# Sparse attention with a gated feed-forward layer on one core: a third unit with seven products, in-place turns, exponentials over two banks, and a newly drawn order

## The chip, the core and the metric

The kernel runs on one core of a Trainium2 chip. The core has five engines with a queue of instructions each: TensorE (PE in the profile) multiplies matrices into PSUM; VectorE (DVE), ScalarE (ACT) and GpSimd (POOL) work on SBUF, the first two on PSUM as well; SyncE (SP) issues transfers. PSUM has eight banks of 512 f32 numbers in each of 128 partitions. An engine takes its instructions strictly in the order of the program and waits on semaphores for the others.

The metric is the time of one execution on the device in microseconds (us). The kernel before was run three times: 274.62, 275.38 and 276.82 us, median 275.38.

## What is computed

Four sequences of 768 rows, eight heads of 64. Queries see chunks of 32 keys. For each query a bound is worked out for every chunk up to its own, from the minimum and the maximum of the chunk's keys; the six chunks with the largest bounds are kept, and a causal softmax over their keys weights the values. The result, as 3072 rows of 512, goes through a gated layer with 1536 hidden columns.

```python
ub = np.sum(np.maximum(q[..., None, :] * k_min, q[..., None, :] * k_max), axis=-1)
top_chunks = np.argsort(np.where(causal, ub, -1e9), axis=-1)[..., -6:]
scores = np.where(selected & (pos[:, None] >= pos[None, :]), scale * q @ k.T, -1e9)
x = softmax(scores) @ v                      # then heads side by side: 3072 x 512
out = (1 / (1 + np.exp(-(x @ w_gate))) * (x @ w_val)) @ w_out
```

## The kernel before

**Units.** The 3072 rows are taken as eight units u0 to u7 of 384 rows, three blocks of 128 each. u1 is blocks 1 to 3 of the first sequence, u2 its blocks 4 and 5 with the first block of the last sequence, u3 blocks 1 to 3 of the second sequence, and so on; u0 collects the first blocks of the others. A unit goes through these steps, whose names stand in the program's list and in this text:

- Keys and queries, loaded as f32. For u1 and u2 they are turned on TensorE (kn, kT, kt, qn, qT, qf). For sequences 1 to 3 they arrive through four transfers (k00_2 or q10_2: tensor, half, half, sequence), already cut into 32 x 32 squares, so that VectorE only has to transpose each square. For the keys (keys_blocks, L839) and each of four pairs of heads: kx0 and kx1 take minimum and maximum of the squares of the raw keys and transpose at once (L684), k16 casts the raw keys to f16 (POOL, L459), kt transposes the cast (L850), and hk0 and hk1 copy the halves to hk, where the scores read them. For the queries (turn_queries, L858) qf0 and qf1 transpose to a tensor of their own (L866); qm takes the positive part, hq0 and hq1 copy to hq (queries_blocks, L870).
- The choice of chunks (choose, L887): ub is the bounds on TensorE into two banks (even and odd heads), and then, for either bank by itself, ubn (transpose), ubm (bar what is not there), mx0/mx1 (eight largest), ap (compare with the sixth), apt (transpose) on VectorE, and hqm copies that add the mask to the query side, so that the score of a dropped chunk comes out very negative.
- Attention (attend, L944): for each of eight heads two to four banks of scores sc, one exponential exp for each bank (ScalarE, L971), the causal cut cm on the diagonal squares (POOL, L977), the values pv on TensorE, then rz (reciprocal) and x (normalise, L1014) on VectorE. x is turned to xT: for u1 and u2 on TensorE with a copy (xps, xT), for u3 to u7 by a transposing transfer.
- The gated layer (ffn, L1234). Hidden columns are taken as three groups of 512. For u0, u1 and u2 each of the twelve column blocks of gate (g) and of value (v) is four products with 384 moving columns (L1247); tanh on ScalarE and hg on VectorE finish the gate. For u3 to u7 (the table SEVEN, L1141) a group is done as a 2 x 2 block product with seven products in place of eight (by7, L1187): products p1 to p7 of four matmuls with 192 columns each (L1199), into two banks, one called lead and one side. e7 copies p7's bank to SBUF, sd copies lead to side, c21 and c22 (L1214) add sums onto the banks, and each quarter goes to tanh or hg. The seven products need sums of weights, ss0 to ss3 for each group (L1170; ss2 overwrites one quarter of the weights, so every plain product with them must have been done), and differences of the unit's input, tt0 to tt3 (L1183).
- The output product: o0, o1, o2 with 512 columns (L1321) for u0 to u3, seven products of two units' blocks (pair, L1063) for u4 to u7, with sums sw of the hidden columns and tw of the output weights (weight_sums, L1042).

**Order.** Nothing is scheduled at run time. The program holds three lists: ORDER (L96) names every step with its engine and is emitted in that sequence, SLOTS (L267) gives each buffer a place in one SBUF tensor called arena, or a PSUM bank, and TIES (L345) makes single steps of POOL wait for the end of a step of VectorE. The list before has 2097 steps, 731 of them on TensorE, 508 on VectorE, 450 on ScalarE, 281 on POOL and 127 on SyncE, and 203 ties. The steps fl are fillers on TensorE in the first microseconds, whose results nobody reads.

Of the kernel before, what the change touches and what calls it, by code (L numbers as in the profile page):

```python
# [14 lines left out]
NEG = -60000.0  # L15
UNITS = 234
# [123 lines left out]
tanh_u1_6=A cm_u2_2=G v_u1_2=P hg_u1_9=V k11_2=S kcr_1=G osb_u0_2=A exp_u2_2_1=A sc_u2_1_2=P exp_u2_0_2=A exp_u2_3_1=A sc_u2_7_1=P  # L140
qf0_u3_1=V k10_2=S sc_u2_6_2=P pv_u2_4=P hq0_u3_0=G exp_u2_6_2=A hg_u1_7=V qf0_u3_2=V pv_u2_5=P v_u1_10=P v_u1_8=P exp_u2_7_1=A qf0_u3_3=V
qm_u3_0=A cm_u2_6=G exp_u2_1_2=A hg_u1_3=V v_u1_6=P hq1_u3_0=G hg_u1_2=V v_u1_11=P hg_u1_6=V hq1_u3_2=G hg_u1_11=V qm_u3_2=A ub_u3=P
hg_u1_8=V k01_2=S xpsf_3_0=P hq0_u3_2=G hk0_1_3=A ss3_g0=G o0_u1_1=P pv_u2_0=P ubn1_u3=V hk1_1_3=A ubn0_u3=V ubm1_u3=V xpsf_3_1=P
xTf_3_1=A kt_1_1=V mx1_u3=V hk1_1_2=A pv_u2_3=P hk0_1_1=A pv_u2_6=P xTf_3_0=A q00_2=S hg_u1_10=V qf0_u4_0=V pv_u2_2=P o1_u1_1=P v16_1_1=G
pv_u2_1=P pv_u2_7=P hk1_1_1=G ap1_u3=V rz_u2_2=V rz_u2_3=V apt1_u3=V rz_u2_0=V hk0_1_0=G x_u2_3=V rz_u2_1=V ubm0_u3=V o2_u1_1=P o0_u1_0=P
x_u2_2=V hk0_1_2=A o1_u1_0=P x_u2_0=V hqm1_u3_2=A q11_2=S osb_u1_1=A xps_u2_3=P sc_u3_7_1=P xT_u2_3=A exp_u3_7_1=A sc_u3_7_2=P mx0_u3=V
qf0_u4_2=V x_u2_1=V hqm1_u3_0=G sc_u3_4_0=P ap0_u3=V exp_u3_4_0=A v16_1_2=G kx1_2_1=V k16_2_3=G xps_u2_2=P apt0_u3=V xT_u2_2=A kx1_2_2=V
sc_u3_5_0=P exp_u3_7_2=A k16_2_0=G hqm0_u3_2=G q01_2=S o0_u1_2=P sc_u3_6_2=P sc_u3_4_2=P exp_u3_4_2=A sc_u3_6_1=P qf0_u4_1=V qf0_u4_3=V
exp_u3_5_0=A o1_u1_2=P k16_2_2=G exp_u3_6_2=A kx0_2_0=V hqm0_u3_0=G sc_u3_5_2=P kt_2_0=V exp_u3_5_2=A exp_u3_6_1=A xps_u2_1=P q10_2=S
sc_u3_6_0=P cm_u3_5=G sc_u3_4_1=P kt_2_3=V exp_u3_6_0=A cm_u3_6=G sc_u3_7_0=P xps_u2_0=P out_u0_1=S o2_u1_0=P xT_u2_1=A kx0_2_2=V  # L150
o2_u1_2=P kx1_2_3=V v_1_3=S xT_u2_0=A g_u2_2=P sc_u3_1_2=P v_1_4=S exp_u3_4_1=A sc_u3_0_1=P g_u2_11=P exp_u3_7_0=A cm_u3_4=G v_1_0=S
cm_u3_7=G sc_u3_5_1=P osb_u1_2=A exp_u3_1_2=A osb_u1_0=A kx0_2_3=V sc_u3_1_0=P k16_2_1=G hk0_2_3=G tanh_u2_11=A v_u2_0=P v_2_1=S
exp_u3_1_0=A cm_u3_1=G exp_u3_0_1=A exp_u3_5_1=A sc_u3_3_1=P qf1_u4_3=V sc_u3_1_1=P exp_u3_1_1=A exp_u3_3_1=A tanh_u2_2=A g_u2_8=P
hk1_2_0=G out_u1_0=S g_u2_10=P qf1_u4_2=V out_u1_1=S kx1_2_0=V qf1_u4_0=V k01_3=S k11_3=S sc_u3_0_2=P v_u2_10=P qf1_u4_1=V sc_u3_3_2=P
g_u2_9=P tanh_u2_10=A hq1_u4_2=G hg_u2_10=V kx0_2_1=V hq0_u4_2=G exp_u3_0_2=A tanh_u2_8=A g_u2_4=P sc_u3_2_1=P v_u2_8=P qf0_u5_1=V
qm_u4_2=A v16_1_3=G v_u2_9=P sc_u3_3_0=P exp_u3_3_2=A hq1_u4_0=G hg_u2_8=V kcr_2=G tanh_u2_9=A out_u0_2=S hg_u2_9=V sc_u3_0_0=P g_u2_0=P
exp_u3_2_1=A qm_u4_0=A g_u2_5=P v16_1_4=G exp_u3_0_0=A qf0_u5_2=V v16_1_0=G ub_u4=P cm_u3_0=G g_u2_3=P exp_u3_3_0=A hk1_2_3=G qf0_u5_3=V
pv_u3_6=P qf0_u5_0=V tanh_u2_0=A k10_3=S tanh_u2_4=A kt_2_1=V sc_u3_2_0=P v16_2_1=G qm_u5_0=A v_u2_11=P ubn0_u4=V tanh_u2_5=A qm_u5_2=A
ubn1_u4=V exp_u3_2_0=A hq1_u5_0=A hk0_2_1=G g_u2_7=P tanh_u2_3=A ubm0_u4=V out_u1_2=S pv_u3_0=P sc_u3_2_2=P exp_u3_2_2=A hg_u2_0=V
mx0_u4=V kt_2_2=V hq1_u5_2=A pv_u3_4=P pv_u3_1=P ap0_u4=V ubm1_u4=V tanh_u2_7=A hg_u2_11=V pv_u3_7=P apt0_u4=V g_u2_1=P v_1_5=S hq0_u4_0=G  # L160
hk1_2_1=G pv_u3_5=P g_u2_6=P tanh_u2_1=A mx1_u4=V k00_3=S hqm0_u4_2=A rz_u3_3=V v_u2_7=P cm_u3_3=G ub_u5=P hg_u2_7=V ap1_u4=V hk0_2_0=G
hk0_2_2=G tanh_u2_6=A x_u3_3=V sc_u4_2_0=P ubn1_u5=V sc_u4_2_2=P apt1_u4=V hqm0_u4_0=A v_u2_4=P v_u2_5=P rz_u3_2=V exp_u4_2_2=A
sc_u4_2_1=P rz_u3_0=V exp_u4_2_0=A sc_u4_1_1=P exp_u4_2_1=A hk1_2_2=G cm_u3_2=G v_u2_1=P hqm1_u4_2=G v_2_0=S ubn0_u5=V hqm1_u4_0=G
sc_u4_3_2=P sc_u4_6_2=P exp_u4_1_1=A x_u3_0=V hg_u2_1=V q10_3=S v_u2_3=P exp_u4_3_2=A cm_u4_2=G sc_u4_5_3=P sc_u4_7_1=P x_u3_2=V
sc_u4_0_0=P pv_u3_3=P exp_u4_6_2=A hg_u2_4=V hg_u2_3=V exp_u4_7_1=A exp_u4_0_0=A sc_u4_6_0=P exp_u4_5_3=A pv_u3_2=P sc_u4_3_1=P v_u2_2=P
sc_u4_3_0=P hg_u2_5=V sc_u4_0_2=P v_u2_6=P exp_u4_3_1=A exp_u4_6_0=A hq0_u5_2=G mx1_u5=V sc_u4_3_3=P sc_u4_4_1=P exp_u4_0_2=A sc_u4_0_1=P
exp_u4_3_3=A hg_u2_2=V sc_u4_5_0=P xT_u3_0=S exp_u4_3_0=A exp_u4_0_1=A sc_u4_4_3=P hg_u2_6=V rz_u3_1=V o0_u2_2=P sc_u4_1_2=P exp_u4_5_0=A
exp_u4_4_1=A sc_u4_5_1=P exp_u4_5_1=A o1_u2_2=P mx0_u5=V ss0_g1=V sc_u4_2_3=P exp_u4_1_2=A sc_u4_4_0=P ss2_g0=G x_u3_1=V ap0_u5=V
xT_u3_1=S sc_u4_1_3=P exp_u4_4_3=A v16_1_5=G sc_u4_1_0=P o0_u2_1=P k16_3_1=A exp_u4_1_3=A kx0_3_2=V sc_u4_7_2=P ss0_g2=V exp_u4_2_3=A
sc_u4_7_3=P k16_3_2=G o1_u2_1=P exp_u4_7_2=A kx1_3_1=V exp_u4_1_0=A xT_u3_3=S ap1_u5=V apt0_u5=V xT_u3_2=S o0_u2_0=P sc_u4_7_0=P ss1_g2=V  # L170
# [230 lines left out]
def kernel(  # L401
# [1065 lines left out]
```

## Time and profile before

| | |
|---|---|
| median of three runs | 275.38 us |
| profiled execution | 274.87 us |
| its span, first to last instruction | 273.0 us |
| busy: PE, DVE, ACT, POOL | 263.1, 227.3, 208.6, 187.3 us |
| idle time of PE | 9.9 us |
| matmuls | 3094 |

The span is what the profile divides into shares; the 1.9 us around it are in the time and not in the profile. In rows of groups the columns are line, engine, operation, output and inputs, shapes and count, then busy time in us, mean ns of one, and the idle time before with what ended it. A matmul's own duration contains the way through the array, so the pace of a stream is read from rows of the chain, where a row gives start, length and the number of products in it.

### The profile page before, as it was taken

How to read it: one execution, taken by the hardware profiler on the slowest of the kernel's cores; microseconds unless marked ns; L12 is line 12 of the kernel's file. 1: busy time of each engine (PE TensorE's matmuls, PEld its weight loads, DVE VectorE, ACT ScalarE, POOL GpSimd, SP SyncE). 2: the span in 40 equal slices, each digit the busy share in tenths (PEclk: the TensorE clock that was granted, in tenths of full speed). 3: DMA queues.
4: the chain of work that ended last, by engine and by line, in shares of the span. 5: the costliest groups of instructions: out<-in, count | busy, mean ns of one | idle time of the engine just before them, and what ended most of it. 6: DMA issues, size and time to landing. Idle time of an engine off the chain costs nothing.

```text
span 273.0 us, 8339 instructions
## 1 busy us (share of the span) xinstructions
PE 263.1 (96%) x3094; PEld 207.8 (76%) x3094; DVE 227.3 (83%) x654; ACT 208.6 (76%) x451; POOL 187.3 (69%) x287
## 2 busy tenths in 40 slices
PE   6979999999999999999999999999999999999994
PEld 4655658657666667675889878899988999999984
DVE  4789846788989989889989999889898879678861
ACT  6378878669886899899889999989998763665322
POOL 5796744658996799697499974887773556584440
PEclk9979999999999999999999999999999999999999
DMA  6999999999999999912783715130200020022035
GB/s 155 240 292 200 204 214 214 214 184 177 170 204 165 202 257 218 180 33 53 166 133 86 195 31 130 42 95 4 46 14 2 17 46 1 2 78 79 2 119 228
DMA packets 131576, 34.74 MB, mean 127 GB/s; under 512 B 119760, under 2 KB 128464, under 8 KB 131536
## 3 DMA queue, kind: packets, MB, share of 16 engines
q1 hardware_dynamic: 126768, 29.50, 50.8%
q0 software_dynamic: 4768, 4.72, 10.2%
q8 instruction: 24, 0.39, 0.6%
q14 instruction: 16, 0.13, 0.1%
HBM read 30.67 MB, written 6.29 MB: 135 GB/s over the span
## 4 chain that ended last, share of the span: by engine, by line
PE 85%; DVE 4%; DMA 4%; ACT 2%; issue 1%; POOL 1%; SPq 1%; DVEq 0%; ACTq 0%
PE sc_u L960 11%; PE g_u L1247 9%; PE o_u L1321 9%; PE v_u L1247 8%; PE pl_v_u L1199 7%; PE pv_u L993 6%; PE pl_g_u L1199 6%; PE pl_u L1092 6%; PE ps_v_u L1199 5%; PE ps_g_u L1199 4%; PE ps_u L1092 4%; PE ube_u L899 3%; DMA arena<-arena 3%; ACT arena L971 1%; DMA arena<-in_k_dram 1%
## 5 line engine op out<-in xcount | busy, mean ns | idle before, releaser
L971 ACT ACTIVATE arena<-sc_u 128x512 f16<-128x512 f32 (+3 forms) x184 | 90.4, 552 | 7.7 <-PE sc_u L960 6.3
L1082 POOL TENSOR_TENSOR arena<-arena 128x256 f16<-128x256 f16 x44 | 29.1, 682 | 23.6 <-DVE arena L1082 9.7
L977 POOL TENSOR_SCALAR_AFFINE_SELECT arena<-arena 128x384 f16<-128x384 f16 (+1 forms) x56 | 28.2, 515 | 18.5 <-DVE arena L1170 4.4
L1321 PE MATMUL o_u<-wo,arena 128*128 128x512 f16 x144 | 35.3, 379 | 0.0
L1199 PEld LDWEIGHTS <-arena 128*128 128x128 f16 x360 | 30.1, 98 | 1.9
L960 PE MATMUL sc_u<-hqe,hke 128*128 128x128 f16 (+2 forms) x220 | 28.9, 243 | 0.0
L1247 PE MATMUL g_u<-arena,wg 128*128 128x384 f16 x144 | 27.5, 326 | 0.9 <-ACT arena L455 0.6
L960 PE MATMUL sc_u<-hqo,hko 128*128 128x128 f16 (+2 forms) x220 | 28.3, 243 | 0.0
L1258 DVE SCALAR_TENSOR_TENSOR arena<-arena,v_u 128x384 f16<-128x384 f16 x36 | 19.2, 549 | 10.1 <-ACT arena L1254 5.6
L1247 PE MATMUL v_u<-arena,wv 128*128 128x384 f16 x144 | 27.2, 326 | 0.0
L993 PE MATMUL pv_u<-v,arena 128*128 128x65 f16 x640 | 26.3, 193 | 0.5 <-DVE arena L1014 0.5
L1092 PEld LDWEIGHTS <-arena 128*128 128x128 f16 x252 | 24.4, 98 | 2.4
L993 PEld LDWEIGHTS <-arena 128*128 128x128 f16 x640 | 24.3, 98 | 2.3 <-issue 0.6
L1321 PEld LDWEIGHTS <-arena 128*128 128x128 f16 x144 | 13.3, 98 | 11.1
L1199 PE MATMUL ps_g_u<-arena,wg 128*128 128x192 f16 x180 | 21.4, 246 | 0.3 <-DVE wg L1170 0.3
L1199 PE MATMUL ps_v_u<-arena,wv 128*128 128x192 f16 x180 | 21.6, 246 | 0.0
L1199 PE MATMUL pl_v_u<-arena 128*128 128x192 f16 x180 | 21.5, 246 | 0.0
L1199 PEld LDWEIGHTS <-wv 128*128 128x128 f16 x240 | 20.0, 98 | 1.8 <-issue 0.6
L1199 PEld LDWEIGHTS <-wg 128*128 128x128 f16 x240 | 20.1, 98 | 1.3 <-DVE wg L1170 0.4
L1199 PE MATMUL pl_g_u<-arena 128*128 128x192 f16 x180 | 21.0, 246 | 0.0
L1247 PEld LDWEIGHTS <-wg 128*128 128x128 f16 x144 | 13.4, 98 | 9.7 <-DMA wg<-in_moe_w_gate_dram 1.6
L1254 ACT ACTIVATE arena<-g_u 128x384 f16<-128x384 f32 x36 | 17.2, 497 | 4.2 <-PE g_u L1247 3.9
(159 smaller groups left out, 666.0 us busy)
## 6 DMA issues: line engine op xcount, KB each, us to landing
arena<-in_v_dram SPq DMA_DIRECT2D x27, 256.0 KB, 4.3
out_dram<-arena SPq DMA_DIRECT2D x24, 256.0 KB, 2.3
arena<-in_k_dram SPq DMA_DIRECT2D x12, 384.0 KB, 5.2
arena<-in_q_dram SPq DMA_DIRECT2D x12, 384.0 KB, 5.5
arena<-in_q_dram SPq DMA_DIRECT2D x12, 128.0 KB, 8.9
arena<-in_k_dram SPq DMA_DIRECT2D x12, 128.0 KB, 4.4
wv<-in_moe_w_val_dram POOLq DMA_DIRECT2D x3, 512.0 KB, 10.0
wo<-in_moe_w_out_dram POOLq DMA_DIRECT2D x3, 512.0 KB, 17.7
```

Of the source, the lines that this page charges most:

```text
L899: nc.tensor.matmul(at(ub[e_])[32 * p:32 * p + 32, lo - u.s0:hi - u.s0], kcr[par][ROWS[e_], p, m, :], at(src)[ROWS[e_], p, lo:hi], start=(m ...
L960: nc.tensor.matmul(at(t)[:, o:o + 128 * m], hk[b % 2][e_][:, p, 128 * jb:128 * jb + 128], hq[u.side][e_][:, p, 128 * x:128 * (x + m)], sta ...
L971: plan.add(f"exp_{u.name}_{h}_{y}", {ACT: act(n)}, lambda e, t=t, att=att, b0=b0, n=n: nc.scalar.activation(at(att)[:, b0:b0 + n], at(t), ...
L977: nc.gpsimd.affine_select(out=dv, in_=dv, compare_op=ALU.is_ge, fill=0.0, base=0, pattern=[[0, u.m], [1, 128]], channel_multiplier=-1)
L993: nc.tensor.matmul(at(pv)[:, last, x, :], at(att)[:, c:c + 128], v16[b % 2][:, jb, h, :], start=(jb == 0), stop=(jb == ib))
L1082: plan.add(f"sw{n}_{name}_{j}", {DVE: dve(256, 2), POOL: pool2(256)}, lambda e, a=a, b=b, op=op, n=n, j=j: both(e).tensor_tensor(sums(n, j ...
L1092: nc.tensor.matmul(at(to), a(j)[:, i], b(j)[:, i], start=first and j == i == 0, stop=j == 2 and i == 1, skip_group_check=True)
L1199: nc.tensor.matmul(at(to)[:, s], a()[:, c, 128 * s:128 * s + 128], b()[:, c], start=first and s == c == 0, stop=c == 1, skip_group_check=True)
L1247: nc.tensor.matmul(at(t), w16[:, c, 128 * fb:128 * fb + 128], at(u.xt)[:, c, :], start=(c == 0), stop=(c == 3))
L1254: plan.add(f"tanh_{u.name}_{name}", {ACT: act(T, psum)}, lambda e: nc.scalar.activation(dst(), src(), AF.Tanh, scale=0.5), reads=reads, wr ...
L1258: plan.add(f"hg_{u.name}_{name}", {DVE: dve(T)}, lambda e: nc.vector.scalar_tensor_tensor(dst(), gate(), 1.0, src(), ALU.add, ALU.mult), r ...
L1321: nc.tensor.matmul(at(o), at(hgs[fc // 2])[:, fc % 2, 128 * tb:128 * tb + 128], wo16[:, fc, lo:hi], start=(fc == 0), stop=(fc == NFB - 1))
```

## The change

- SEVEN gets an entry for u2, all three groups of gate and value. The weight sums ss are then made before u2, and its plain blocks g_u2 and v_u2 go.
- keys_blocks transposes the raw f32 keys in place, two pairs of heads at a time (kt, 1536 columns), takes minimum and maximum of the result without a transpose, and hk0/hk1 cast and copy from it. k16 and the separate f16 buffer go. turn_queries turns the raw queries in place, two pairs at a time; qm and hq read them there, by segment of a unit. So k1, k2, k3 and q1, q2, q3 stay in their places until the last copy has read them.
- choose puts both halves of the bounds of u3 to u7 into two neighbouring banks and has one ubn, ubm, ap and apt for both.
- attend, for u2 to u7 (MERGED): two banks of scores that lie side by side in PSUM get one exponential of up to 1024 columns. An odd last bank keeps its own.
- PSUM is one tensor of eight banks, cut by the places of SLOTS.
- tw, the sums of output weights, are made behind u4's gates and not before u1, and one of them overwrites a quarter of the output weights, so u0 to u3's output products come before it. The sums sw likewise use one block of the hidden columns as it is.
- ORDER, SLOTS and TIES are new from the first loads of k1 on (SLOTS everywhere): 2005 steps, 749 on TensorE, 470 on VectorE, 396 on ScalarE, 263 on POOL, 127 on SyncE, and 158 ties. There are 120 exponentials in place of 184.

The diff, cut to its core:

```diff
+MERGED = (2, 3, 4, 5, 6, 7)
...
+    bank = banks.tile([128, 8 * 512], F32, tag="bank", name="bank")
...
-        for p in range(NP):
-            extremes(par, f"{b}", p, lambda p=p: at(raw)[:, p], S, every, kx, slice(0, NC), blocks, True, next_)
-            k16 = Buf("np", f"k16_{b}_{p}", [128, NC, CH], F16)
-            kt = Buf("np", f"kt_{b}_{p}", [128, S], F16)
...
+        for p in range(0, NP, 2):
+            ps_ = (p, p + 1)
+            plan.add(f"kt_{b}_{p}", {DVE: dve(2 * S)}, lambda e, p=p: nc.vector.transpose(
+                flat(at(raw)[:, p:p + 2]), flat(at(raw)[:, p:p + 2])), reads=[(raw, i) for i in range(4)],
+                writes=[(raw, "turned", p)], prio=next_())
...
+            def turn(e, p=p):
+                t = flat(at(raw)[:, p:p + 2, c0:c0 + 4 * m])
+                nc.vector.transpose(t, t)
...
-                t = ps(f"sc_{u.name}_{h}_{y}", "sc", [128, n])
+                wide = u.i in MERGED and y // 2 * 2 + 1 < nb
...
+                elif y % 2 == 0:
+                    assert n == 512
+                    t2 = ps(f"sc2_{u.name}_{h}_{y}", "sc", [128, 512 + 128 * sum(w[3] for w in u.banks[y + 1])])
...
+                plan.add(f"exp_{u.name}_{h}_{ys[0]}", {ACT: act(n)}, lambda e, t=t, att=att, b0=b0, n=n: nc.scalar.activation(
+                    at(att)[:, b0:b0 + n], at(t)[:, 0:n], AF.Exp, scale=scale), reads=tks, writes=[(att, z) for z in ys], prio=next_())
...
-    SEVEN = {3: {"g": (0, 1, 2), "v": (0, 1, 2)}, 4: {"g": (0, 1, 2), "v": (0, 1, 2)}, ...
+    SEVEN = {2: {"g": (0, 1, 2), "v": (0, 1, 2)}, 3: {"g": (0, 1, 2), "v": (0, 1, 2)}, ...
...
+        if u.i == PAIRED[0]:
+            weight_sums(base)
...
-    weight_sums(0.4)
```

The part of the new ORDER around u2's products, for VectorE alone: x_u2_3, kt_2_2, kt_2_0, kx0_2_2, kx0_2_0, kx1_2_2, kx1_2_0, c21_g0_u2, qf0_u5_0, hg_u2_000, c22_g0_u2, c21_v0_u2. For SyncE, behind k2's four loads: q01_2, v_1_3, v_1_1, v_1_0, q11_2, q00_2, q10_2. Among the ties is tt3_u2<kx1_2_2.

More of the change, by code (lines that the diff above doesn't have):

```diff
@@ L143 @@
[L143 to L150, printed above, removed]
@@ L155 @@
[L155 to L158, printed above, removed]
@@ new lines @@
+p1_g2_u2=P v_2_0=S v_1_2=S ss2_v2=G v_1_4=S p1_g1_u2=P osb_u1_0=A sd_v0_u2=A p7_g2_u2=P p2_v0_u2=P v16_1_0=G p4_g0_u2=P qf0_u5_0=V
+p5_g0_u2=P p6_v0_u2=P e7_g1_u2=A hg_u2_000=V sd_g1_u2=A tanh_u2_010=A c22_g0_u2=V e7_g2_u2=A sd_g2_u2=A p2_g1_u2=P sc_u3_7_2=P kcr_2=G
+hk0_2_2=G p6_g1_u2=P v16_1_2=G c21_v0_u2=V tanh_u2_100=A v16_1_4=G p3_g0_u2=P qf1_u4_2=V p2_g2_u2=P exp_u3_7_2=A qf1_u4_0=V c21_g1_u2=V
+p5_v0_u2=P c22_v0_u2=V out_u1_1=S p6_g2_u2=P tanh_u2_001=A tanh_u2_200=A sc_u3_0_1=P v16_2_0=G sc_u3_0_0=P c21_g2_u2=V p4_g1_u2=P
@@ L434, in at @@
     def at(b):
-        if b.tile is None and b.kind == "ps":
-            b.tile = banks.tile(b.shape, b.dtype, tag=f"{b.kind}{b.slot}", name=b.name)
         if b.tile is None:
@@ L824, in queries_wide @@
         u.qm = Buf("qm", f"qm_{u.name}", [128, NP, T])
-        u.turned = [(u.qf, p) for p in range(NP)]
+        u.read = [(u.qf, p) for p in range(NP)] + [(u.qm, p) for p in range(NP)]
+        u.view = lambda s, p: at(u.qf)[:, p, 0:u.t]
         for p in range(NP):
@@ L887, in choose @@
-    def choose(u, next_):
-        ub = [ps(f"ub{'eo'[e]}_{u.name}", "ub", [128, u.n]) for e in range(2)]
+        u.raw = getattr(u, "raw", []) + [(raw, c0)]
+        for p in range(0, NP, 2):
+            def turn(e, p=p):
+                t = flat(at(raw)[:, p:p + 2, c0:c0 + 4 * m])
+                nc.vector.transpose(t, t)
+            plan.add(f"qf{seg}_{u.name}_{p}", {DVE: dve(256 * m)}, turn, reads=[(raw, i) for i in range(4)],
+                     writes=[(raw, u.name, p)], prio=next_())
@@ L931, in choose @@
[L931 to L941 removed]
+        halves_ = [("", slice(0, 2), (0, 1))] if both_ else [(e, slice(e, e + 1), (e,)) for e in range(2)]
```

659 lines of the change are left out of this document (342 added, 317 removed).

## Prediction

> **What bounds the kernel now.** I read the clock and the page's busy shares first, then busy time by stretches, then the chain that ended last for the pace of each kind of product, and last the waits of TensorE.
>
> ```profile
> core 0: 273.0 us, clock 0.994
> PE 263.1 (96%) x3094; PEld 207.8 (76%) x3094; DVE 227.3 (83%) x654; ACT 208.6 (76%) x451; POOL 187.3 (69%) x287
> PE   6979999999999999999999999999999999999994
> ```
>
> ```profile
> 22.00:130.00 108.00, 107.14 (x1109) 69.29 (x1108) 91.85 (x292) 90.52 (x200) 78.86 (x125) 1.00 1.00 180
> 130.00:145.00 15.00, 14.25 (x210) 12.95 (x208) 14.04 (x31) 13.26 (x31) 10.85 (x14) 1.00 0.79 155
> 145.00:270.00 125.00, 124.55 (x1649) 113.18 (x1647) 105.63 (x294) 91.80 (x203) 80.27 (x118) 1.00 0.21 60
> ```
>
> The columns behind the length of a stretch are the busy time (and instructions) of PE, weight loads, DVE, ACT, POOL, then the clock. From 22 us to 270 us TensorE is idle for 0.86 + 0.75 + 0.45 = 2.06 us in all, at full clock. The rest of its 9.9 us of idle time lies in the first 22 us and behind its last product. A busy PE could still be a slow PE, so I check the pace:
>
> ```profile
> 94.91 0.65 PE g_u L1247 x4
> 149.01 0.66 PE ps_v_u L1199 x8
> 171.65 0.86 PE o_u L1321 x4
> 102.78 0.45 PE sc_u L960 x8
> ```
>
> Four products of 384 columns take 0.65 us, eight of 192 take 0.66, four of 512 take 0.86: 0.42 to 0.43 ns a column in each, so they stand back to back. The kernel is bound by the columns that TensorE has to stream. A change gains what it takes off them, gains at most 2.06 us more from gaps behind 22 us, and loses what new gaps it opens. The two longest gaps between 130 and 145 us are these, both ended by VectorE:
>
> ```profile
> 131.65 0.42 PE L1199 MATMUL ps_g_u<-arena,wg 128*128 128x192 f16 x3 [0.27 <-DVE wg L1170]
> 141.12 0.46 PE L993 MATMUL pv_u<-v,arena 128*128 128x65 f16 x10 [0.48 <-DVE arena L1014]
> ```
>
> The first is a weight sum for u3's products, the second a normalised output of u4. 0.27 + 0.48 = 0.75 us, all that this stretch loses.
>
> **The change, part by part.** *Seven products for u2.* Before, one group of four column blocks of gate or value costs 4 x 0.65 = 2.60 us. With seven products of four matmuls of 192 columns (0.33 us each, half of the row of eight) it is 7 x 0.33 = 2.31 us. u2 has three groups of gate and three of value: 6 x 0.29 = 1.74 us less, straight on the path. It is the only part that takes columns off TensorE; scores, bounds, attention values and output products keep theirs.
>
> ```profile
> L1214 DVE TENSOR_TENSOR ps_v_u<-pl_v_u,arena 128x384 f32<-128x384 f32 x15 | 8.4, 559 | 1.3 <-PE pl_v_u L1199 0.9
> L455 ACT COPY ps_g_u<-pl_g_u 128x384 f32<-128x384 f32 x12 | 5.5, 468 | 2.0 <-PE pl_g_u L1199 0.7 <-ACT arena L1059 0.6 <-ACT arena L455 0.5
> L1183 POOL TENSOR_TENSOR arena<-arena 128x384 f16<-128x384 f16 x11 | 10.0, 911 | 1.7 <-DVE arena L1258 0.9 <-DVE arena L1082 0.5 <-DVE arena L1012 0.2
> L1170 POOL TENSOR_TENSOR arena<-wv,arena 128x512 f16<-128x512 f16 x3 | 3.5, 1156 | 0.1
> ```
>
> The other engines pay: 12 sums onto PSUM on VectorE (c21, c22), 12 x 0.56 = 6.7 us; 12 copies on ScalarE (e7, sd), 12 x 0.47 = 5.6 us; four differences tt of u2's input on POOL, 3.6 us. The 24 weight sums are made once either way, but must now be ready one unit earlier, and POOL takes 19 of them where it took 15: 4 x 1.16 = 4.6 us.
>
> *Keys and queries turned in place, two head pairs at a time.*
>
> ```profile
> L850 DVE STREAM_TRANSPOSE arena<-arena 128x768 f16<-128x768 f16 x12 | 11.3, 951 | 0.0
> L684 DVE TRANSPOSE_TENSOR_REDUCE arena<-arena 128x24 f32<-128x768 f32 x12 | 11.2, 949 | 0.0
> L866 DVE STREAM_TRANSPOSE arena<-arena 128x384 f32<-128x384 f32 x12 | 6.1, 549 | 0.0
> L459 POOL CAST arena<-arena 128x768 f16<-128x768 f32 x11 | 9.0, 823 | 1.2 <-PE sc_u L960 0.7 <-DVE arena L1258 0.3
> ```
>
> From 384 to 768 columns a VectorE pass grows from 549 to 949 ns, 1.04 ns a column, in f32 and f16 alike. So 1536 columns are 949 + 768 x 1.04 = 1750 ns, an estimate. Transposes of keys: 12 x 0.95 becomes 6 x 1.75, 0.9 us less; minima and maxima: 24 x 0.95 becomes 12 x 1.75, 1.8 us less; queries halve 28 instructions, about 14 x 0.15 = 2.1 us less; the bounds' 15 merged instructions about 2.2 us. Against the 6.7 us above, VectorE stays even at about 227 us. POOL loses eleven casts (11 x 0.82 = 9.0 us) and gets the 4.6 us and nine more tt (8.2 us): even too. None of it is on TensorE's path in the mean; what it costs there is where a queue is late (below).
>
> *One exponential per two banks.*
>
> ```profile
> L971 ACT ACTIVATE arena<-sc_u 128x512 f16<-128x512 f32 x120 | 67.9, 605 | 3.5 <-PE sc_u L960 2.7
> L971 ACT ACTIVATE arena<-sc_u 128x128 f16<-128x128 f32 x8 | 2.3, 314 | 0.6 <-PE sc_u L960 0.5
> ```
>
> The slope is (605 - 314) / 384 = 0.76 ns a column, the fixed part 217 ns. 184 instructions become 120: 64 x 0.217 = 13.9 us off ScalarE, less the 5.6 us above. ScalarE had 17 us free of 108 between 22 and 130 us, so this is hidden behind TensorE; I count 0. A pair of 1024 columns takes 993 ns where the first half was done after 605, 0.39 us later for whoever waits on it. That is covered because the causal cut and the values stand many products behind the scores; uncovered, it would be 0.39 us at a place. Whether one instruction across two banks keeps the slope is not in the trace: between 0.99 us and twice 605, and even the worse end only gives ScalarE its old load back.
>
> *Order, places, output weight sums.* The list is the same up to the first loads of k1, so the first 22 us stay but for other PSUM places of the fillers: 0, within plus or minus 0.3 us. The output weight sums move behind u4's gates; u0 to u3's output products must now be done before one of them overwrites wo: 0, since u4's pairs come some 20 us of products later. SyncE keeps its 127 instructions, but the loads move:
>
> ```profile
> 82.67 0.52 DVE L910 STREAM_TRANSPOSE arena<-ubo_u 128x320 f32<-128x320 f32 x1 [0.31 <-PE ubo_u L899]
> 82.73 8.38 SPq L660 DMA_DIRECT2D arena<-in_q_dram  x4
> 93.94 3.43 SPq L670 DMA_DIRECT2D arena<-in_v_dram  x4
> 97.85 0.47 DVE L866 STREAM_TRANSPOSE arena<-arena 128x128 f32<-128x128 f32 x2
> arena<-in_q_dram SPq DMA_DIRECT2D x12, 384.0 KB, 5.5
> L455 ACT COPY hko<-arena 64x1536 f16<-64x1536 f16 x2 | 2.9, 1467 | 0.0
> ```
>
> q2's raw queries were loaded once u3's bounds were done (82.6 us), issued in 8.38 us, first turned at 97.85 us: ample. Now k1 itself is read until its last copies to hk, and q2 lies in its place. Those two copies (hk0_1_0, hk0_1_2, 1.47 us each, on ScalarE) are listed right behind u3's bounds. Then come q2's four loads with three of v1 among them, 8.4 + 3 x 0.86 = 11.0 us, and 5.5 us to landing: 2.9 + 11.0 + 5.5 = 19.4 us. From u3's bounds to qf0_u5_0, the first turn of q2, the new list holds 17.7 us of products. So it comes up to 1.7 us late. Behind it on VectorE stand hg_u2_000, c22_g0_u2 and c21_v0_u2, and u2's p5_v0 waits for the last; TensorE has 2.1 us of products from p5_g0 to there, VectorE needs 2.3 for the turn (0.95) and the three sums, so a delay passes on in full. Ends: 0 (SyncE issues faster with k2 already in) and 1.7; neither is nearer, I take 0.9.
>
> *Sum.* The profiled execution took 274.87 us (span 273.0 and 1.9 around it), 0.5 below the median of 275.38. -1.74 + 0.9 = -0.84: 274.03 against its own time, 274.5 against the median. The 0.75 us of gaps I leave in, since other sums and outputs will be late in their place.
>
> **The rivals.** *Slower: VectorE's queue in front of u2's products.* Six passes over k2 of 1.75 us, 0.08 less each where they overlap, 10.0 us in a row, stand in the new list between x_u2_3 (u2's last normalised output) and c21_g0_u2. p5_g0_u2 waits for that sum. From xps_u2_3 to p5_g0_u2 TensorE has five output parts (4.3 us), twelve products (4.0), eleven scores (2.1) and a turn (0.1): 10.5 us. 10.0 + 0.56 leaves nothing over. POOL's tt3_u2 also holds for the fifth of the six (kx1_2_2), with weight sum ss2_v2 and two casts queued behind it. For it: VectorE was 94% busy from 130 to 145 us and ended both gaps there. Against it: k2 is loaded early, so the first pass can start at once. If it starts only where the list has it, 3.6 us of products later, TensorE waits 3.6 us: 274.5 + 3.6 = 278.1. From 0.84 us of such waits on the kernel is slower than before, from 3.6 on by over 1%.
>
> *Faster: the gaps go too.* q2 lands in time (0), the 0.75 us between 130 and 145 us vanish because u3's weight sums are made a unit earlier, and half of the 0.86 us before: 275.38 - 1.74 - 0.75 - 0.4 = 272.5. Against it: the same engines carry the same load, in a list as tight.
>
> *The seven products give nothing: weight loads pace them.*
>
> ```profile
> L1199 PEld LDWEIGHTS <-arena 128*128 128x128 f16 x360 | 30.1, 98 | 1.9
> ```
>
> 28 loads of 98 ns would be 2.74 us a group, over the 2.60 of the whole form: 6 x 0.14 = 0.9 us lost instead of 1.74 won, 275.38 + 0.9 = 276.2. Against it speaks the row of eight in 0.66 us: 82 ns a product, load included. The Trainium skill, TensorE: Matmul & The Clock Gate, section Back-to-back issue gap, states that weight loads set the pace of a sustained stream together with the products, some 81 ns at 128 columns and 131 at 512. Between them, an estimate from that page, 192 columns would take 89 ns, a group 2.50 us, and the gain would be 0.6 us, the time 275.7 with the late load. The trace does not agree: 82 ns at 192 columns, 56 at 128 (eight scores in 0.45 us).
>
> **How the numbers follow.** A measurement of this kernel tells about 1% from no change: below 272.6 is faster, above 278.1 slower. Forecast 0.55 (its own range 273.4 to 275.5: the load at 0 or 1.7, and 0.2 around); slower rival 0.30, of it 0.17 above 278.1, since several such queues can add up; faster rival 0.12, of it 0.11 below 272.6; weight loads 0.03. Faster 0.11, same 0.72, slower 0.17. Range 272.4 to 278.4, which leaves about 0.08 below and 0.12 above.
>
> **What would show it.** Right: in the profile after, 72 more matmuls, PE busy about 1.7 us less, u2's products at 0.66 us for eight; exponentials of 1024 columns near 1.0 us; TensorE's waits between 80 and 130 us naming VectorE or a transpose of q2, 1 to 2 us in all. Wrong: several us of gaps there, or exponentials of 1.2 us, or products of u2 above 90 ns each; or a span well below 271.3, which would mean that time before 22 us moved, on which I count nothing.

## The result, and the profile after

The changed kernel takes 273.74 us (median of nine runs, 273.41 to 275.55) where the kernel before, nine runs beside it, takes 275.38: a ratio of 0.9944 with a 95% interval of 0.9918 to 0.997, or 1.5 us less, between 0.8 and 2.3. Forecast were 274.5 us and a change too small to tell from none by the 1% bound. The profiled execution took 274.43 us with a span of 272.7. First the clock and the busy shares, then the same three stretches as in the prediction (PE, weight loads, DVE, ACT, POOL, clock).

```profile
core 0: 272.7 us, clock 0.987
PE 262.4 (96%) x3166; PEld 213.4 (78%) x3166; DVE 226.2 (83%) x612; ACT 209.0 (77%) x397; POOL 182.2 (67%) x269
```

```profile
22.00:130.00 108.00, 107.41 (x1195) 75.61 (x1194) 94.77 (x271) 95.56 (x187) 81.26 (x116) 0.99 1.01 182
130.00:145.00 15.00, 15.00 (x233) 13.64 (x232) 13.33 (x21) 13.71 (x28) 14.39 (x21) 1.00 0.89 167
145.00:270.00 125.00, 123.15 (x1623) 111.86 (x1619) 102.88 (x284) 86.51 (x165) 69.15 (x103) 1.00 0.21 61
```

There are 72 more matmuls, as forecast. Between 130 and 145 us TensorE is never idle, where 0.75 us of idle time showed before. The last stretch can't be read by its idle time, since the products end inside it: at 268.2 us here, and at 269.55 before, so that the 0.45 us which the prediction counted there as a gap lay behind the last product. The span is only 0.3 us shorter, since this execution was slow at both ends. To see that, I cut every execution at two steps of TensorE that all kernels have: ub_u2, the bounds of u2 (the first row of each pair below, before and then after), and p3z_u67, the last product, 0.39 us before the end of the second row.

```profile
55.82 0.40 PE L899 MATMUL ube_u<-arena,kcr 64*32 64x256 f32 x1
...
268.73 0.82 PE L1092 MATMUL pl_u<-wo,arena 128*128 128x256 f16 x6
```

```profile
57.31 1.09 PE L904 MATMUL bank<-arena,kcr 64*32 64x256 f32 x32
...
266.02 2.13 PE L1127 MATMUL bank<-wo,arena 128*128 128x256 f16 x18
```

Starts of those steps from the trace of each execution, in us; "middle" is from the start of ub_u2 to the start of p3z_u67:

| execution | ub_u2 at | middle | p3z_u67 to the end |
|---|---|---|---|
| before | 55.82 | 213.35 | 3.82 |
| before, a second time (e11) | 57.34 | 213.06 | 3.83 |
| after | 57.31 | 210.45 | 4.95 |
| e1, 24 matmuls more | 56.37 | 212.42 | 4.28 |
| e2, 24 matmuls fewer | 56.68 | 209.78 | 4.17 |
| e3, exponentials split | 57.99 | 210.52 | 4.90 |
| e4, no ties | 58.18 | 214.80 | 5.00 |
| e6, q2 late | 57.95 | 210.93 | 4.97 |
| e7, two k2 passes twice | 57.18 | 213.25 | 4.99 |
| e8, before, tie and swap | 56.29 | 214.97 | 3.81 |
| e9, ten fillers more | 57.80 | 210.46 | 4.30 |
| e10, before, swap alone | 57.19 | 213.96 | 3.81 |
| e12, VectorE passes added | 59.47 | 214.76 | 5.00 |

The middle repeats to 0.07 us over after, e3 and e9, and to 0.3 in the kernel before. The change takes 2.9 us off it (2.6 against e11). The first 57 us scatter by 1.5 us and more in one and the same order. The end, behind the last product, is 0.35 to 1.2 us longer in all nine executions of the new order.

### The profile page after: what moved, and what is told of

It reads as the page before. It is cut to its first block, busy times and chain, and to the rows that moved or that the text cites. A ratio compares the mean times of both kernels' runs of the same rounds, so it can differ in the third digit from the quotient of the medians.

```text
span 272.7 us, 8361 instructions
## 1 busy us (share of the span) xinstructions
PE 262.4 (96%) x3166; PEld 213.4 (78%) x3166; DVE 226.2 (83%) x612; ACT 209.0 (77%) x397; POOL 182.2 (67%) x269
## 4 chain that ended last, share of the span: by engine, by line
PE 83%; DMA 6%; DVE 3%; SPq 3%; issue 1%; ACT 1%; POOL 1%; DVEq 0%; POOLq 0%
PE bank L1234 31%; PE bank L983 12%; PE bank L1358 11%; PE bank L1127 10%; PE bank L1022 7%; PE bank L1282 7%; DMA wg<-in_moe_w_gate_dram 5%; PE bank L904 3%; SPq L621 2%; PE bank L780 2%; DMA arena<-in_k_dram 1%; DVE arena L439 1%; ACT arena L1000 1%; PE bank L576 1%; PE bank L760 0%
## 5 line engine op out<-in xcount | busy, mean ns | idle before, releaser
L1000 ACT ACTIVATE arena<-bank 128x1024 f16<-128x1024 f32 (+5 forms) x120 | 84.3, 750 | 5.7 <-PE bank L983 4.4
L1234 PE MATMUL bank<-arena 128*128 128x192 f16 x432 | 50.6, 246 | 0.0
L1293 DVE SCALAR_TENSOR_TENSOR arena<-arena,bank 128x384 f16<-128x384 f16 x78 | 41.4, 543 | 10.4 <-ACT arena L1289 5.1
L1289 ACT ACTIVATE arena<-bank 128x384 f16<-128x384 f32 x78 | 37.4, 493 | 8.9 <-PE bank L1234 4.9
L1358 PE MATMUL bank<-wo,arena 128*128 128x512 f16 x144 | 36.0, 379 | 0.0
L1234 PE MATMUL bank<-arena,wv 128*128 128x192 f16 x288 | 34.0, 246 | 0.0
L1234 PE MATMUL bank<-arena,wg 128*128 128x192 f16 x288 | 32.6, 246 | 0.0
L1022 PE MATMUL bank<-v,arena 128*128 128x65 f16 x640 | 27.0, 194 | 0.0
L983 PE MATMUL bank<-hqo,hko 128*128 128x128 f16 (+2 forms) x220 | 26.6, 244 | 0.0
L983 PE MATMUL bank<-hqe,hke 128*128 128x128 f16 (+2 forms) x220 | 26.4, 244 | 0.0
L437 ACT COPY arena<-bank 128x384 f32<-128x384 f32 (+3 forms) x44 | 19.4, 451 | 5.9 <-PE bank L1234 2.7
```

Source lines behind the costliest of these rows:

```text
L437: nc.scalar.copy(o, i)
L983: nc.tensor.matmul(at(t)[:, o:o + 128 * m], hk[b % 2][e_][:, p, 128 * jb:128 * jb + 128], hq[u.side][e_][:, p, 128 * x:128 * (x + m)], sta ...
L1000: plan.add(f"exp_{u.name}_{h}_{ys[0]}", {ACT: act(n)}, lambda e, t=t, att=att, b0=b0, n=n: nc.scalar.activation(at(att)[:, b0:b0 + n], at( ...
L1022: nc.tensor.matmul(at(pv)[:, last, x, :], at(att)[:, c:c + 128], v16[b % 2][:, jb, h, :], start=(jb == 0), stop=(jb == ib))
L1234: nc.tensor.matmul(at(to)[:, s], a()[:, c, 128 * s:128 * s + 128], b()[:, c], start=first and s == c == 0, stop=c == 1, skip_group_check=True)
L1289: plan.add(f"tanh_{u.name}_{name}", {ACT: act(T, psum)}, lambda e: nc.scalar.activation(dst(), src(), AF.Tanh, scale=0.5), reads=reads, wr ...
```

## The experiments

**e1 and e2: columns.** In the loop over a product's matmuls:

```diff
-                for s in range(2):
+                for again in range(2 if u.i == 2 and p == "p1" else 1):      # e1, then the loop as it was
+                for s in range(0 if u.i == 2 and p == "p3" else 2):          # e2
```

> The changed kernel with product p1 of each of u2's six groups made twice, the second time over the first: 6 x 4 = 24 more matmuls of 192 columns with their weight loads. Theory (the time follows the columns that TensorE streams, one for one): 6 x 0.33 = 1.98 us more, 273.74 becomes 275.7, and u2's gain is gone. Rival (queues of the other engines set the pace at u2, and the new order brought the gain): less than 0.8 us more, 274.5 or below.

Measured: 274.97 us, ratio 0.9989 (0.9962 to 1.0017), middle 212.42. 1.97 us more for 24 matmuls is 82 ns each, weight load included. The theory's 1.98, in the part of the trace that repeats; the times say 1.2 us more than the change, with intervals that hold 2. The weight loads do not pace these products. The Trainium skill, TensorE: Matmul & The Clock Gate, section Wait — 56ns, not 53.3ns?, gives columns over 2.4 GHz and 2.5 ns as the pace of a warm stream, an estimate of 82.5 ns for 192 columns. This trace agrees with that, and not with the 89 ns that the prediction estimated from the section Back-to-back issue gap.

> The changed kernel without product p3 of u2's six groups (u2's gate and value miss that term): 24 matmuls of 192 columns fewer. Theory: 1.98 us less, 271.8; VectorE's sums keep up, because c21_g0_u2 was done 0.8 us before TensorE came to p5_g0_u2. Rival (VectorE or POOL becomes the bound in u2): at most 1 us less, 272.7 or above, with waits of TensorE for VectorE between 95 and 125 us.

Measured: 272.66 us, ratio 0.9905 (0.9868 to 0.9942), middle 209.78: 0.67 us less, not 1.98 (the times say 1.1). That is the rival's size and not its cause. No wait of TensorE above 0.2 us shows up; from start to start of its products, eight pieces of 0.08 to 0.18 us between 101 and 118 us, 1.2 us together, make up nearly all that is missing. In the trace six of them end with a step of ScalarE and two with one of VectorE; the rival had named VectorE and POOL. Columns added cost in full. Columns taken off give back only what the other queues can follow, and in u2 the new list leaves them little.

**e3: the merged exponential.**

```diff
-nc.scalar.activation(at(att)[:, b0:b0 + n], at(t)[:, 0:n], AF.Exp, scale=scale)
+[nc.scalar.activation(at(att)[:, b0 + lo:b0 + min(n, lo + 512)], at(t)[:, lo:min(n, lo + 512)], AF.Exp, scale=scale)
+ for lo in range(0, n, 512)]
```

> The changed kernel with each of the 64 exponentials over two banks issued as two instructions of up to 512 columns, in the same place: 64 x 0.217 = 13.9 us more on ScalarE, 209 becomes 223 of 272. Theory (ScalarE is off the path, the merged exponential gives nothing to the time): 273.7 to 274.3. Rival (the new order lives on the free time that merging gave ScalarE): some 7 of the 13.9 us fall between 22 and 130 us, where ScalarE has 12 us free in scattered pieces, and 2 us or more reach TensorE: 275.7 or above.

Measured: 274.28 us, ratio 0.9947 (0.9923 to 0.9971), middle 210.52. Merging gives nothing to the time. But my price for it was wrong as well. The busy line of the split kernel, and the merged instruction in the changed one:

```profile
PE 261.3 (96%) x3166; PEld 212.2 (78%) x3166; DVE 226.4 (83%) x612; ACT 210.8 (77%) x461; POOL 181.9 (67%) x269
```

```profile
L1000 ACT ACTIVATE arena<-bank 128x1024 f16<-128x1024 f32 x40 | 40.4, 1023 | 2.0 <-PE bank L983 1.3
```

64 more instructions make ScalarE busy for 210.8 us where it was 209.0: 0.03 us each, not 0.217. The 217 ns were read from durations of single instructions; on a queue that is full, the next one starts inside them (in the split kernel an exponential of 512 columns takes 621 ns, and its second half starts 477 ns after the first). One instruction over two banks took 1023 ns; 993 were forecast.

**e4: without ties.** The list TIES is left empty.

> The changed kernel without its 158 ties: POOL's steps start as soon as their data is there, beside VectorE's. Theory (the time is TensorE's columns, VectorE has 46 us free): within 1 us of 273.7, either way. Rival (keeping VectorE and POOL apart is what keeps VectorE's queue in step): VectorE's and POOL's passes get longer where they overlap, their busy sums grow by over 10 us, and TensorE's waits for them cost 2 us or more: 275.7 or above.

Measured: 278.52 us, ratio 1.0101 (1.0063 to 1.0139), middle 214.80, 4.35 us more. The rival holds. Groups of VectorE passes, first with ties, then without (the line numbers shift by 21):

```profile
L1293 DVE SCALAR_TENSOR_TENSOR arena<-arena,bank 128x384 f16<-128x384 f16 x78 | 41.4, 543 | 10.4 <-ACT arena L1289 5.1 <-PE bank L1234 2.7 <-ACT arena L1094 1.2
L831 DVE STREAM_TRANSPOSE arena<-arena 128x1536 f32<-128x1536 f32 x6 | 10.4, 1754 | 0.0
L1293 DVE SCALAR_TENSOR_TENSOR arena<-arena 128x384 f16<-128x384 f16 x18 | 10.3, 586 | 0.0
L1117 DVE TENSOR_TENSOR arena<-arena 128x256 f16<-128x256 f16 x33 | 8.4, 285 | 0.1
```

```profile
L1272 DVE SCALAR_TENSOR_TENSOR arena<-arena,bank 128x384 f16<-128x384 f16 x78 | 41.4, 543 | 8.2 <-ACT arena L1268 4.6 <-ACT arena L1073 1.2 <-PE bank L1213 1.2
L1272 DVE SCALAR_TENSOR_TENSOR arena<-arena 128x384 f16<-128x384 f16 x18 | 13.8, 780 | 0.0
L1096 DVE TENSOR_TENSOR arena<-arena 128x256 f16<-128x256 f16 x33 | 12.7, 414 | 0.1
L810 DVE STREAM_TRANSPOSE arena<-arena 128x1536 f32<-128x1536 f32 x6 | 10.3, 1747 | 0.0
```

Passes with two inputs in SBUF get a third to a half longer beside POOL (586 to 780 ns, 285 to 414). Those with one input in PSUM (543) or with one input only (1754 and 1747) do not. The Trainium skill, SBUF — State Buffer, section Who interferes with whom, says that a VectorE instruction with two SBUF inputs contends with a GpSimd instruction that reads SBUF, because its second input comes through the read interface that the two share, and that one with at most one SBUF input, outside the modes with two ports, does not. The two groups that stretch and the two that don't agree with it. TensorE then waits for VectorE:

```profile
PE bank L1213 <- DVE bank L1228: 1.6, 2, 1.1
PE bank L1001 <- DVE arena L1022: 0.9, 1, 0.9
```

**e6: q2 late.** One tie more: q11_2<o1_u1_1.

> The changed kernel with the second of q2's four loads held until an output product of u1 is done (91.9 us in the profile of the changed kernel, where it was issued at 88.65): q2 lands 3.25 us later, some 101.9 us in place of 98.6, and qf0_u5_0, which ran at 100.17, starts 1.7 us late. Theory (behind qf0_u5_0 nothing on VectorE covers a delay but 0.53 us, which is how long c21_v0_u2 was done before p5_v0_u2): the stretch from u2's bounds to the last product grows by 1.2 us or more, the time to about 274.9. Rival (a late q2 is hidden): 0 to 0.2 us.

Measured: 274.35 us, ratio 0.9946 (0.9924 to 0.9968), middle 210.93, 0.48 us more. VectorE's queue in the changed kernel, and then in this one:

```profile
99.70 0.56 DVE L1249 TENSOR_TENSOR bank<-bank,arena 128x384 f32<-128x384 f32 x1 [0.28 <-PE bank L1234]
100.17 0.97 DVE L853 STREAM_TRANSPOSE arena<-arena 128x768 f32<-128x768 f32 x1
```

```profile
100.33 0.57 DVE L1249 TENSOR_TENSOR bank<-bank,arena 128x384 f32<-128x384 f32 x1 [0.28 <-PE bank L1234]
101.68 0.98 DVE L853 STREAM_TRANSPOSE arena<-arena 128x768 f32<-128x768 f32 x1 [0.78 <-DMA arena<-in_q_dram]
```

The last load landed at 101.49 us in place of 98.59. VectorE waited 0.78 us for it and TensorE 0.48 from start to start, at p3_g0_u2. So the delay does pass on, less than in full; 1.2 us was too much. Here VectorE started 0.19 us behind the landing; with that, some 1.4 us (98.78 to 100.17) are to spare in the changed kernel.

**e7: VectorE's queue in front of u2's products.**

```diff
-nc.vector.tensor_reduce(out=outs[m](), ...)
+[nc.vector.tensor_reduce(out=outs[m](), ...) for again in range(2 if b == 2 and m == 0 else 1)]
```

> The changed kernel with both minimum passes over k2 (kx0_2_2 and kx0_2_0) made twice: 2 x 1.66 = 3.3 us more on VectorE ahead of c21_g0_u2. Theory (the slower rival's price: VectorE's queue in front of u2's products has 0.8 us to spare at p5_g0_u2, and what goes beyond reaches TensorE): 3.3 - 0.8 - 0.3 that VectorE waited itself = 2.2 us, the time near 275.9, with one wait of TensorE at p5_g0_u2. Rival (VectorE's 46 us of free time take it up): under 0.5 us, below 274.3.

Measured: 277.87 us, ratio 1.0079 (1.0046 to 1.0111), middle 213.25: 2.8 us more, forecast 2.2. The times say 3.7 more than the change, with intervals that hold 2.8. VectorE's rows and the wait of TensorE:

```profile
92.60 6.94 DVE L836 TENSOR_REDUCE kcr<-arena 128x48 f32<-128x1536 f32 x4
99.46 3.40 DVE L836 TENSOR_REDUCE arena<-arena 128x48 f32<-128x1536 f32 x2
102.78 0.56 DVE L1249 TENSOR_TENSOR bank<-bank,arena 128x384 f32<-128x384 f32 x1
```

```profile
PE bank L1234 <- DVE bank L1249: 2.6, 1, 2.6
```

3.3 us of VectorE in the wrong place cost 2.8 us of the kernel, though VectorE is idle for 46 us elsewhere. The slower rival's way of pricing holds, and the price was a little higher.

**e5 and e9: the clock in the first 25 us.** Ten fillers more (fl_30 to fl_39) behind qfT_2.

> The changed kernel with ten more fillers on TensorE behind qfT_2, where TensorE was idle for 1.18 us (13.45 to 14.63 us), and some 2 us later the granted clock was 0.5 until 23.5 us: 10 x 0.11 = 1.1 us of work that nobody reads. Theory (the idle time lets the clock go): clock 1.00 in every stretch from 15 to 26 us, and 0.3 to 1 us less, 272.8 to 273.4. Rival (loads and POOL set the first 25 us, whatever the clock): 273.5 to 274.0, whether the clock stays or not.

Measured: 273.68 us, ratio 0.9908 (0.9868 to 0.9947). In its profiled execution a product of attention values waited 4.6 us, in the end for a load of v that took 23.5 us to land, so only the times are used.

> The run with ten more fillers again, now into the PSUM bank of pvf_0_0, which has been read by then (in the run before they overwrote kfT_0, which is still read at 14.7 us, so minimum and maximum of the first keys were wrong). Theory (1.18 us without work lets the clock go): granted clock 1.00 from 15 to 26 us, the first product of u0's gate (24.42 us in the changed kernel) 0.5 to 1 us earlier, the time 272.8 to 273.4. Rival (loads set the first 57 us whatever the clock: u0's fifth gate product waited 0.5 to 5 us for its weights in some of the runs): u2's bounds come at 56.4 to 58.0 as in the other runs, the time 273.5 to 274.0.

Measured: 273.57 us, ratio 0.9923 (0.9896 to 0.995). Three stretches of the changed kernel and then of this one (clock in the third column from the end):

```profile
15.00:20.00 5.00, 4.10 (x35) 2.91 (x35) 4.02 (x13) 3.95 (x8) 4.54 (x9) 0.64 1.11 271
20.00:22.00 2.00, 2.00 (x15) 1.88 (x14) 1.43 (x4) 1.35 (x3) 2.00 (x4) 0.50 1.20 197
22.00:24.00 2.00, 2.00 (x15) 1.84 (x14) 1.21 (x4) 1.13 (x4) 0.62 (x3) 0.68 1.22 196
```

```profile
15.00:20.00 5.00, 2.98 (x34) 2.21 (x35) 3.77 (x13) 4.10 (x8) 4.21 (x8) 1.00 1.10 259
20.00:22.00 2.00, 2.00 (x23) 1.66 (x22) 1.73 (x5) 1.23 (x4) 2.00 (x5) 1.00 1.22 201
22.00:24.00 2.00, 1.40 (x11) 0.96 (x11) 2.00 (x5) 1.97 (x6) 1.85 (x5) 1.00 1.22 196
```

The clock stays at 1.00, the theory's first half. The second half fails: ub_u2 starts at 57.80 us, the middle is 210.46, and the time cannot be told from the change's. What TensorE gains in pace it loses in waits: between 5 and 57 us they add up to 5.4 us here and to 3.5 in the changed kernel, and most of the difference is waits for POOL. (The waits of u0's gate products for their weights, 0.5 to 5 us in the expectation, are at most 1.4 us in these traces.) The fillers are not needed for the clock: e1, e3 and e4 had 1.00 from 15 to 22 us without them. Over all fourteen traces it goes with the work before: in the nine whose clock fell to 0.5 within 18 us, TensorE was busy for 0.64 to 0.86 of the 2 us between 13 and 15 us; in the five where it stayed at 1.00 to 24 us, for 1.06 to 1.94. u2's bounds came no sooner in those five (56.4 to 61.9 us) than in the nine (55.8 to 59.5).

**e8 and e10: the two gaps of the kernel before.** The first was VectorE's weight sum ss2_g1 beside POOL's ss2_v0 (first VectorE's row, then POOL's):

```profile
130.22 1.37 DVE L1170 TENSOR_TENSOR wg<-wg 128x512 f16<-128x512 f16 x1
```

```profile
130.15 1.15 POOL L1170 TENSOR_TENSOR arena<-arena,wv 128x512 f16<-128x512 f16 x1
```

The expectations below put the second down to the order of VectorE's steps. The chain that ended last shows a transfer in its place: x_u4_0 is written to the place in the arena that x_u4_1 had (105 in SLOTS), and waits until the transposing transfer has read it.

```profile
136.40 4.01 DMA arena<-arena
140.50 0.57 DVE arena L1014
141.12 0.55 PE pv_u L993 x13
```

e8 adds the tie ss2_v0<ss2_g1 to the kernel before, and both kernels swap two steps of VectorE:

```diff
-rz_u4_0=V exp_u5_3_2=A kx0_3_1=V ... x_u4_0=V
+rz_u4_0=V exp_u5_3_2=A x_u4_0=V kx0_3_1=V ...
```

> The kernel before with its two gaps between 130 and 145 us mended: a tie makes POOL's weight sum ss2_v0 wait for VectorE's ss2_g1, which took 1.37 us beside it where such a sum takes 0.40, and x_u4_0 stands ahead of kx0_3_1 on VectorE. Theory (each gap has one cause of its own, so a list can lose both): the stretch from u2's bounds to the last product, 213.35 us, loses 0.6 to 0.75, and the time goes from 275.4 to about 274.7. Rival, as the prediction had it (other sums and outputs are late in their place): 213.1 to 213.4, and the time does not move.

Measured: 277.67 us, ratio 1.0074 (1.0046 to 1.0103), middle 214.97: 1.6 us more. TensorE's waits between 128 and 146 us are these:

```profile
PE ps_g_u L1199 <- POOL arena L1183: 1.6, 1, 1.6
PE pv_u L993 <- POOL arena L977: 0.6, 1, 0.6
```

Neither of the old gaps shows, and POOL, which the tie held for 6.9 us, brings two new ones. x_u4_0 still waits 2.04 us for its transfer, but TensorE, held up ahead of it, comes to that product later.

> The kernel before with the swap alone: x_u4_0 ahead of kx0_3_1 on VectorE, no new tie. In the run with both, the two gaps were gone and POOL's queue, held 6.9 us for VectorE, brought two others of 0.6 and 1.6 us. Theory (the tie did that, the swap is free): the stretch from u2's bounds to the last product 212.9, 0.48 below the 213.35 of before. Rival (any mend in a list this tight opens another gap): 213.2 or more.

Measured: 276.54 us, ratio 1.0027 (1.0003 to 1.0051), middle 213.96, 0.6 more. The swap is not free either:

```profile
139.94 0.17 DVE L1012 RECIPROCAL arena<-pv_u 128x6 f32<-128x6 f32 x1
141.95 0.56 DVE L1014 TENSOR_TENSOR arena<-pv_u,arena 128x384 f16<-128x384 f32 x1 [1.84 <-DMA arena<-arena]
```

x_u4_0 waits 1.84 us for that transfer. Before, the pass over k3 that stood ahead of it filled 0.92 us of this time, and it waited for the other 0.93. So the swap could not close the second gap, which is still there, and it moved VectorE's work back.

**e11: the kernel before again.**

> The kernel before, unchanged, for a second look at its first 57 us and its end. Theory (the new places cost nothing ahead of u2's bounds; what varies there is the landing of loads): u2's bounds start between 55.8 and 58.2 us, as they do over the runs of the changed kernel; from u2's bounds to the last product 213.3 to 213.4; 3.8 us from the last product to the end. Rival (the start of the kernel before is faster by a us): 55.8 to 56.3.

Measured: one run, 276.11 us; ub_u2 at 57.34, middle 213.06, end 3.83. The start of the kernel before scatters like that of the changed one (55.8 to 57.3 against 56.4 to 59.5); a difference of half a us between the two would not show. The middle was 0.3 us shorter than expected: the gap at 141 us was 0.37 in place of 0.64 from start to start, and the transfer ahead of it took 3.75 us in place of 4.01.

**e12: VectorE's load put back.** Behind each of eight steps of VectorE:

```diff
+        for half in range(2 if op.name in AGAIN else 0):
+            nc.vector.tensor_tensor(ident32[:, :].bitcast(F16), wg16[:, 0, 0:256], wg16[:, 1, 0:256], ALU.add)
```

What it puts back is this: weight sums between 122 and 145 us, VectorE and then POOL, in the kernel before and in the changed one.

```profile
122.00:145.00 23.00, 4.67 (x8) 9.21 (x8) 1.00 0.61 120
```

```profile
122.00:145.00 23.00, 0.00 (x0) 0.00 (x0) 1.00 0.77 146
```

> The changed kernel with 16 f16 passes of 256 columns more on VectorE, two behind each of eight of its steps between 122 and 136 us (results that nobody reads): 16 x 0.285 = 4.6 us, what the kernel before spent there on VectorE for u3's and later units' weight sums (4.67 us). Theory (the two gaps between 130 and 145 us went because those sums are made before u2 now): twelve passes, 3.4 us, stand ahead of c21_g0_u3, VectorE waited 0.93 us there itself and was done 1.35 us before p5_g0_u3, so 1.1 us or more reach TensorE: 211.2 us or above from u2's bounds to the last product, where the changed kernel has 210.45. Rival (VectorE has room there all the same, the gaps went for the other order): 210.4 to 210.7.

Measured: one run, 281.03 us; middle 214.76, 4.3 us more than the changed kernel. Four waits of TensorE return, two ended by VectorE and two by POOL, the longest these:

```profile
PE bank L1234 <- DVE bank L1249: 1.4, 1, 1.4
PE bank L983 <- POOL hqe L441: 0.7, 1, 0.7
```

The eight added pairs took 7.1 us together in place of 4.6, three of them 1.1 to 1.3 us each in place of 0.57, and POOL's ties wait for the lengthened steps. So VectorE has no room for these passes there; the size isn't a clean price of 4.6 us.

## Why the prediction came out

**What bounds the kernel: right.** TensorE's columns count one for one (e1), and the rest shows only where a queue is late. The 2.06 us of idle time behind 22 us were 1.61, since 0.45 of them lay behind the last product.

**Seven products for u2, -1.74 us: right** as a count of columns, by the pace of e1. e2 adds a limit that the prediction did not have: another 1.98 us of columns taken off u2 brought 0.67.

**q2 late, +0.9: wrong size, it was 0.** The step that failed is "2.9 + 11.0 + 5.5 = 19.4 us", counted from u3's bounds. It took the copies hk0_1_0 and hk0_1_2 to begin where the list has them, behind the bounds. ScalarE had run ahead and ended them at 84.10 us, 0.75 behind the end of the bounds and not 2.9. SyncE's rows after:

```profile
84.12 0.31 SPq L642 DMA_DIRECT2D arena<-in_q_dram  x1
84.53 4.00 SPq L652 DMA_DIRECT2D arena<-in_v_dram  x3
88.65 5.53 SPq L642 DMA_DIRECT2D arena<-in_q_dram  x3
```

The seven issues took 10.1 us for 11.0 reckoned, and the last landed at 98.59, 4.4 us behind its issue for 5.5 reckoned. That makes 0.75 + 10.1 + 4.4 = 15.2 us, where 16.8 passed from the bounds' end to qf0_u5_0. The mechanism is there (e6).

**The gaps, left in at 0.75: wrong, they went, and they had cost more than 0.75.** These rows of the kernel before stand just ahead of its two waits:

```profile
130.82 0.55 PE L993 MATMUL pv_u<-v,arena 128*128 128x65 f16 x13
140.25 0.38 PE L960 MATMUL sc_u<-hqe,hke 128*128 128x384 f16 x2
```

Thirteen products of 65 columns need 0.39 us at their pace of 0.03, so the next could have started at 131.21 us and did at 131.65. A score of 384 columns and one of 128, the second in its row, need 0.22 us, so the next could have started at 140.47 and did at 141.12. That is 0.44 and 0.64 us, 1.08 together. The idle time shows 0.27 and 0.48 of it, because a product counts as busy until it has left the array. So of the 2.9 us off the middle 1.74 are columns, and the other 1.15 are nearly all these two gaps (0.9 against e11). "Other sums and outputs will be late in their place" is what befell the order of before in e8 and e10, but not the new one. In it the weight sums were made between 59 and 113 us, and 122 to 145 us holds none, so the stretched sum of the first gap is not there; e12 shows that VectorE had no room for passes in their place. The second gap went for another reason: x_u4_0 takes the place of x_u4_1 in the new list too, but stands nine steps of VectorE behind it and starts 6.4 us later (143.04 against 136.60; before, 140.50 against 135.82), without waiting for the transfer. The whole list was drawn anew besides, and e4 puts 4.35 us on its ties.

**The end: a term that was missing.** From the last product to the end it is 0.35 to 1.2 us more. Stores in the last us took this long to land, before and after:

```profile
out_dram<-arena SPq DMA_DIRECT2D x3, 256.0 KB, 2.0
```

```profile
out_dram<-arena SPq DMA_DIRECT2D x2, 256.0 KB, 2.8
```

In e1, e2 and e9 they landed in 2.0 us with the new order too, and the end was still 0.35 to 0.5 longer, behind the last landing. Why is open.

**The start, 0 within 0.3: not resolved**, since it scatters by more than that. The list is the same up to u2's bounds; they come at 56.7 us in the mean of the four executions of the order before and at 57.6 in the seven that share the change's steps up to there.

**Load of the engines.** VectorE was put at 227 us and has 226.2; passes over 1536 columns were put at 1750 ns and take 1754, 1743 and 1726. ScalarE was put at 208.6 - 13.9 + 5.6 = 200.3 and has 209.0: the step "64 x 0.217 = 13.9" failed (e3), at no cost, since it was counted as hidden. POOL was called even, though its own terms (4.6 + 8.2 - 9.0) add up to 3.8 us more; it has 182.2 where it had 187.3, and why isn't shown.

**The sum.** -1.74 - 1.15 + 0.35 to 1.2 is -2.5 to -1.7, and the runs say -2.3 to -0.8 with the scatter of the start in it. Forecast was -0.84. That the range held the time is in part luck: q2's 0.9 and the gaps' 1.15 were wrong towards slow, and the end, which was missing, took 0.35 to 1.2 of that back.

**The signs.** The 72 matmuls, the exponentials near 1.0 us and the pace of u2's products came as said. TensorE's waits between 80 and 130 us, 1 to 2 us in all, did not come. TensorE's busy time fell by 0.7 us and not by 1.7, since the first 57 us took 1.4 more; in the middle alone it fell from 212.60 to 210.45.

**The rivals.** The slower one did not occur: the first of the six passes began 0.33 us after x_u2_3 began (89.38 against 89.05), not 3.6 us later, and the sum was ready 0.8 us before p5_g0_u2. Its way of pricing held (e7). The faster one had q2 in time and came out on the 2.9 us of the middle (1.74 + 0.75 + 0.4). That is in part luck: its 0.4 was meant for idle time ahead of 130 us, all of which lay ahead of u2's bounds, and what came in its place is that the two gaps were larger than shown. The end, and perhaps the start, took part of the gain back. Weight loads pace nothing (e1).

A version clearly better than both isn't among these runs: e9 has the lowest ratio with the full computation, 0.9923, but its interval overlaps that of the change.

## What to carry to other kernels

Where one engine is busy for 96% of the span, cut the execution at two of its steps that every variant has: the middle repeated to 0.07 us here, to 0.3 in the worst case, while the whole time scattered by two, so effects of half a us could be told apart. Ask of each queue how much it has to spare at the place that waits, not how idle it is in the mean: VectorE had 46 us free, and 3.3 us more in the wrong place cost 2.8. Read the cause of a gap from the chain and not from the order of the list, and mend it only with the other queues in view: a tie for a real cause and a swap for one that was not the cause cost 1.6 us here.

## What the runs showed of the hardware

- VectorE passes with two SBUF inputs stretch beside POOL: one sum of 128x512 f16 took 1.37 us where 0.40 is usual, and without ties VectorE is busy for 238.3 us in place of 226.2.
- Back-to-back instructions of ScalarE cost only 0.03 us more when an exponential is cut in two, though a single one has a fixed part of 0.2 us by the durations at 512 and 128 columns (605 and 314 ns).
- In the changed kernel TensorE idled from 13.45 to 14.63 us, and the granted clock was 0.5 from 16.4 to 23.3 us. With fillers in that gap it stayed at 1.00, as it did in three runs without them where TensorE had more to do between 13 and 15 us, and the kernel was no faster for it.
